# Attention scores masked before the exponential, from a score bank and an SBUF tile

## The chip, the cores and the metric

The kernel runs on one core of a Trainium2 chip. The metric is the device time of one execution in microseconds (us), the median of three runs.

## The reference, cut to what matters

```
scores = (1 / sqrt(64)) * q @ k.T                       # 4 batches, 8 heads, 576 x 576, head size 64
thresh = max(scores, axis=-1) - tau                     # tau = 0.02
scores = where(scores >= thresh, scores, -1e9)
attn   = exp(scores - max(scores))
attn   = attn / (sum(attn, axis=-1) + 1e-9)
x      = attn @ v                                       # then as 2304 x 512
x      = (silu(x @ w_gate) * (x @ w_val)) @ w_out       # inner size 1536
out    = ((x @ w1) * (x @ w2) @ w3) @ w_out2            # inner size 1024
```

All data are float32 (the weights come as 64-bit numbers). Products are made as sums of three matmuls over a high and a low part of each operand.

## The kernel before, in words

The function `attention` goes over 16 pairs of heads (4 batches x 4 pairs, `p`), and over 9 tiles `i` of 128 query rows by 576 keys in each, 144 tiles in all: tiles 0 to 3 are of the first head, 5 to 8 of the second, and tile 4 holds the last 64 rows of both. A loop over all tiles (L705) writes the stages of several tiles into each turn:

- `mm_scores` (L426): TensorE (PE) writes the scores of tile n + 2 into one of two score banks (`s_bank`, L91), with 4 matmuls (8 for tile 4).
- `el_max` (L475): VectorE (DVE) reads the bank of tile n + 1, multiplies by -1 (the operand `neg`), writes the negative scores to the tile's piece of `P` in SBUF and keeps the minimum, which is minus the row maximum, in `stat`. With this the bank is free.
- `el_thr` (L466): GpSimd (POOL) adds tau to these minima, for two tiles at a time in most cases.
- `el_exp` (L485): ScalarE (ACT) makes `E` = exp(score - max) from `P`; three buffers `E`.
- `el_mask` (L494), two tiles later (`N_THR`): DVE writes (P <= threshold) x E to `P` and the row sums to `sums`.

Between these, `some` (L693) spreads items of two queues. `main` holds the work on finished tiles: transposes of `P` on PE (`it_T`, `it_lq`, `it_kl`, `it_corner`, with `turn_p` at L326) and their split into a high and a low part (`evac_split`, L506, by one of three paths: with a subtraction on DVE at L520, with one by matmul on PE at L333, or with POOL at L101 and L104), and the value matmuls (`it_pv`, L569, matmuls at L579 and L584). `prep` holds the transposes of q and k for the next pair (`it_k`, `it_q`, `it_left`; the copies at L341 and L311, the low parts on DVE at L343); 0.125, the scale of the scores, goes into q there and, for the first pair, in `first` (L383). In pairs 3, 6 and 9 and in the last pair, conversion of weights (`conv_step`, L140 to L200) and loads of x come in too.

This order is not yet the order on an engine. The kernel is built with a scheduler (`schedule_with_timeline_sim`) that sorts the instructions of each engine by when it takes them to be ready; on the chip each engine then keeps its sorted order and waits on semaphores.

After the attention come the two feed-forward parts: conversion of weights, `glu_step` and the bilinear part, with nearly all matmuls at L830.

## Time and profile before

| | us |
|---|---|
| median of 3 runs | 1183.39 (1183.26 to 1184.7) |
| span of the profiled execution | 1178.8 |
| lowest run less this span | 4.5 |
| PE busy | 1113.3 (94%) |
| DVE busy | 750.1 (64%) |
| ACT busy | 578.1 (49%) |
| POOL busy | 439.7 (37%) |

The profile shows one execution. Its span is from the first to the last instruction; what lies around it is seen in the runs alone, and the lowest run stands in for the profiled execution's own time, which is not listed apart. PE is TensorE's matmuls, PEld its weight loads, SP the engine that issues DMAs. The shares are means over the whole span, in which the attention and the feed-forward parts differ. In the trace's rows an instruction stands as output<-inputs, with its line; a number in brackets, or after a bar, is the idle time of the engine before it and what ended that. PEclk is the granted TensorE clock as a share of full speed.

### The profile page before, as it was taken

Reading aid. Unit: us, or ns where it says so; the run is one execution under the profiler, and the core shown is the slowest. Engines: PE = TensorE matmul, PEld = TensorE weight load, DVE = VectorE, ACT = ScalarE, POOL = GpSimd, SP = SyncE. Lnnn points to the kernel's source line nnn. Section 1 sums busy time; section 2 is a strip of 40 time slices with the busy share of each in tenths; the row PEclk is TensorE's granted clock in tenths of the full one; section 3 lists DMA queues with packets and bytes.
Section 4 is the critical chain, followed back from the end, with each engine's and each line's share of the span. In section 5 each row is a group of like instructions: output and inputs, shape, how many; then the busy total and the mean of one; then the engine's idle time right before and its main releaser. Section 6 shows DMA issues by size and latency. Waiting matters only on the chain.

```text
span 1178.8 us, 16730 instructions
## 1 busy us (share of the span) xinstructions
PE 1113.3 (94%) x6044; PEld 952.0 (81%) x6044; DVE 750.1 (64%) x1320; ACT 578.1 (49%) x1041; POOL 439.7 (37%) x431
## 2 busy tenths in 40 slices
PE   6898879899988899999999999999899999999998
PEld 5787769788876778888888888888787888888886
DVE  7999898999886786665472655477891122522222
ACT  5787876888876455443232433344662231321111
POOL 4365454555444555443241432333242221321110
PEclk9999999999999999999999999999999999999999
DMA  8865674766555832221120120123330010100023
GB/s 189 194 146 131 145 177 112 167 147 137 121 175 141 257 99 87 89 72 55 35 71 19 54 72 19 52 92 102 113 108 18 1 36 1 36 1 1 1 60 101
DMA packets 105330, 107.07 MB, mean 91 GB/s; under 512 B 48288, under 2 KB 79648, under 8 KB 105248
## 3 DMA queue, kind: packets, MB, share of 16 engines
q1 hardware_dynamic: 105104, 106.01, 34.2%
q8 instruction: 47, 0.77, 0.3%
q14 instruction: 35, 0.29, 0.1%
q10 hardware_dynamic: 144, 0.00, 0.0%
HBM read 68.16 MB, written 14.23 MB: 70 GB/s over the span
## 4 chain that ended last, share of the span: by engine, by line
PE 64%; DVE 19%; DMA 8%; issue 3%; POOL 2%; SPq 2%; ACT 2%; DVEq 0%; ACTq 0%; POOLq 0%
PE t_bank L830 36%; PE s_bank L830 19%; DVE P L498 5%; DVE P L479 4%; PE t_bank L579 4%; PE s_bank L440 2%; DMA raw<-in_moe_w_dram 2%; DMA slot<-x_dram 1%; PE t_bank L326 1%; DVE slot L813 1%; DMA slot<-r_dram 1%; DVE tmp L158 1%; DVE tmp L146 1%; DVE AT L520 1%; DMA L<-qlo 1%
## 5 line engine op out<-in xcount | busy, mean ns | idle before, releaser
L830 PE MATMUL t_bank<-slot,slot 128*128 128x512 f32 (+1 forms) x2592 | 559.9, 371 | 5.6 <-DVE slot L813 1.8
L830 PEld LDWEIGHTS t_bank<-slot,slot 128*128 128x128 f32 x2592 | 457.5, 189 | 91.7 <-DVE slot L813 2.7
L830 PE MATMUL s_bank<-h,slot 128*128 128x512 f32 (+1 forms) x720 | 161.0, 371 | 7.4 <-DVE slot L877 4.2
L151 POOL TENSOR_TENSOR raw<-raw 128x512 int32<-128x512 int32 x76 | 83.9, 1104 | 189.0 <-ACT raw L150 165.3
L830 PEld LDWEIGHTS s_bank<-h,slot 128*128 128x128 f32 x720 | 126.4, 190 | 31.9 <-ACT tmp L914 3.2
L498 DVE SCALAR_TENSOR_TENSOR P<-P,stat,E 128x576 f32<-128x576 f32 x144 | 142.0, 999 | 11.8 <-POOL stat L471 10.6
L1062 DVE TENSOR_TENSOR tmp<-tmp,t_bank 128x512 f32<-128x512 f32 (+1 forms) x40 | 25.4, 634 | 178.3 <-PE t_bank L830 178.3
L488 ACT ACTIVATE E<-P,stat 128x576 f32<-128x576 f32 x144 | 113.6, 791 | 27.9 <-DVE P L479 25.2
L108 POOL TENSOR_TENSOR h<-tmp,h 128x512 fp32r<-128x512 f32 (+1 forms) x60 | 74.5, 1242 | 128.8 <-ACT h L107 128.6
L479 DVE TENSOR_SCALAR_CACHE_REDUCE P<-s_bank,neg 128x576 f32<-128x576 f32 x144 | 115.0, 808 | 10.3 <-PE s_bank L440 9.8
L1066 POOL TENSOR_TENSOR h<-tmp,h 128x512 fp32r<-128x512 f32 (+1 forms) x38 | 45.8, 1206 | 200.8 <-ACT h L1064 200.8
L440 PE MATMUL s_bank<-R,L 128*128 128x288 f32 x512 | 100.0, 317 | 19.3 <-DVE P L479 12.6
L830 PE MATMUL s_bank<-slot,h 128*128 128x512 f32 x432 | 106.6, 391 | 0.9 <-DVE slot L1052 0.8
L915 DVE TENSOR_TENSOR tmp<-tmp,t_bank 128x512 f32<-128x512 f32 (+1 forms) x60 | 37.9, 631 | 107.2 <-PE t_bank L830 100.5
L440 PEld LDWEIGHTS s_bank<-R,L 128*128 128x128 f32 x512 | 74.6, 191 | 33.8 <-DVE P L479 24.2
L326 PE MATMUL t_bank<-ident,P 128*128 128x128 f32 x640 | 91.4, 279 | 6.3 <-DVE klo L343 1.3
L830 PEld LDWEIGHTS s_bank<-slot,h 128*128 128x128 f32 x432 | 79.9, 188 | 18.3 <-DVE slot L1052 2.1
L158 DVE SCALAR_TENSOR_TENSOR tmp<-tmp,raw 128x512 f32<-128x512 f32 x76 | 69.5, 915 | 39.3 <-POOL raw L151 39.3
L877 DVE TENSOR_TENSOR slot<-s_bank,slot 128x1024 f32<-128x1024 f32 (+1 forms) x72 | 82.5, 1147 | 18.5 <-PE s_bank L830 16.5
L149 ACT ACTIVATE raw<-raw,ebias 128x512 int32<-128x512 int32 x76 | 58.0, 764 | 61.9 <-DVE tmp L146 48.2
L914 ACT ACTIVATE tmp<-t_bank 128x512 f32<-128x512 f32 (+1 forms) x60 | 33.3, 555 | 110.0 <-PE t_bank L830 104.3
L326 PEld LDWEIGHTS t_bank<-ident,P 128*128 128x128 f32 x640 | 74.3, 142 | 13.6 <-DVE klo L343 2.0
(103 smaller groups left out, 1397.8 us busy)
## 6 DMA issues: line engine op xcount, KB each, us to landing
raw<-in_moe_w_dram SPq DMA_DIRECT2D x32, 512.0 KB, 3.6
raw<-in_moe_w_out_dram SPq DMA_DIRECT2D x20, 512.0 KB, 3.6
x_dram<-xs SPq DMA_DIRECT2D x64, 144.0 KB, 2.4
L<-qlo SPq DMA_DIRECT2D x60, 128.0 KB, 2.4
...
```

Of the source, the lines that this page charges most:

```text
L108: nc.gpsimd.tensor_tensor(out=lo, in0=src, in1=f32(hi), op=ALU.subtract)
L149: nc.scalar.activation(out=a, in_=x, func=ACTF.Relu, scale=8.0, bias=ebias[:, 0:1])
L151: nc.gpsimd.tensor_tensor(out=a, in0=a, in1=x, op=ALU.subtract)
L158: nc.vector.scalar_tensor_tensor(out=f32(m), in0=f32(m), scalar=2.0 ** 20, in1=f32(a), op0=ALU.add, op1=ALU.mult)
L326: nc.tensor.matmul(bank[:, t * P:(t + 1) * P], lhsT=part, rhs=ident, is_transpose=True, start=(t == 0), stop=(t == len(parts) - 1),)
L440: nc.tensor.matmul(o, lhsT=lhs, rhs=R[:, c:c + HALF], start=(h == hs2[0] and e == 0), stop=(h == hs2[-1] and e == 1),)
L479: nc.vector.tensor_scalar(out=p_tile(p, i).rearrange("p (a c) -> p a c", a=2), in0=sb[:, :, 0:HALF], scalar1=neg, scalar2=None, op0=ALU.mu ...
L488: nc.scalar.activation(out=e, in_=p_tile(p, i), func=ACTF.Exp, scale=-1.0, bias=stats[p // HP][:, 0, c:c + 1],)
L498: nc.vector.scalar_tensor_tensor(out=t, in0=t, scalar=stats[b][:, 1, c:c + 1], in1=e, op0=ALU.is_le, op1=ALU.mult, accum_out=sums[b][:, c: ...
L579: nc.tensor.matmul(o, lhsT=vs[:, 4 * h + c, :, :].rearrange("p a d -> p (a d)"), rhs=AT[h][:, e, c, cs], start=(c == 0 and e == 0), stop=F ...
L830: nc.tensor.matmul(o, lhsT=lhs(a), rhs=rhs(c), start=(first and i == 0), stop=(last and i == 2))
L877: nc.vector.tensor_tensor(out=a, in0=s, in1=a, op=ALU.add)
```

## The change

- The scale 0.125 that goes into q becomes 0.125 / 1024 (`q_scale`, 0 where tau is negative), and is read from SBUF instead of being a constant. The score banks hold scores / 1024.
- `el_max`, `el_thr`, `el_exp` and `el_mask` give way to one function, `el_tile`, of four instructions in one chain. DVE multiplies the bank by -1024 into an SBUF tile (named `E`, two buffers) and keeps the minimum (L473). DVE adds tau to it (L477, 128x1). DVE compares the SBUF tile with that threshold and subtracts the bank from the result of 0 or 1, into `P` (L481): -s for what is kept, 1 - s for what is not, in units of 1024. ACT makes exp(-1024 x P - max), in place, which is 0 for what is not kept, and gives the row sums (L485).
- The bank is read last by L481. POOL has no part in this any more.
- A turn of the loop has `some(0.5)`, the tile, the scores of tile n + 2, `some(0.5)`. Work on a finished tile enters its queue in the turn of the tile, and not two turns later.

```diff
--- before.py
+++ after.py
@@ -19,7 +19,8 @@
 
 PASSES = ((0, 0), (0, 1), (1, 0))
 
-N_THR, N_E = 2, 3
+N_E = 2
+FAR = 1024.0
 
 N_U1, N_U2, N_U3, N_U4 = 3, 6, 9, 24
 N_TMP, N_BIG, N_HB = 6, 3, 3
@@ -85,7 +86,7 @@
     ident_r = const.tile([P, P], F32R, name="ident_r")
     minus_r = const.tile([P, P], F32R, name="minus_r")
     tau_sb = const.tile([P, 1], F32, name="tau_sb")
-    neg = const.tile([P, 1], F32, name="neg")
+    q_scale = const.tile([P, 1], F32, name="q_scale")
     ebias = const.tile([P, 2], F32, name="ebias")
 
     def s_bank():
@@ -360,7 +361,7 @@
                 stack(L[:, 2, :], hi, lo, 0)
                 stack(L[:, 3, :], lo, hi, 1)
 
-            turn(raws.pop((p, 0)), hi, lo, 0.125, then)
+            turn(raws.pop((p, 0)), hi, lo, q_scale, then)
 
         def it_k(p):
             L, R = qk_tiles(p)
@@ -418,7 +419,7 @@
                     nc.tensor.transpose(br[:, c:c + P], src, ident_r)
             lz = LZ.rearrange("p e (h c) -> p e h c", c=192)[:, :, :, 0:64]
             bv = bank.rearrange("p (e h c) -> p e h c", e=2, h=2)
-            scaled(lz, bv[:, :, :, 0:64], 0.125)
+            scaled(lz, bv[:, :, :, 0:64], q_scale)
             scaled(R[:, 512:640].rearrange("p (h c) -> p h c", h=2), bv[:, 1, :, 64:P])
             scaled(R[:, 2 * S:2 * S + 64], bv[:, 1, 1, 64:P])
 
@@ -463,41 +464,27 @@
                 sums[b] = wk.tile([P, NSM], F32, tag="sums", name="sums")
             return stats[b]
 
-        def el_thr(p, i):
-            st = stats[p // HP]
-            if i in (0, 2, 5, 7):
-                return
-            c = slice(col_of(p, i) - (i != 4), col_of(p, i) + 1)
-            nc.gpsimd.tensor_scalar(
-                out=st[:, 1, c], in0=st[:, 0, c], scalar1=tau_sb, scalar2=None, op0=ALU.add
-            )
-
-        def el_max(p, i, sb):
-            b = p // HP
-            st = stat(b)
-            c = col_of(p, i)
+        def el_tile(p, i, sb):
+            st = stat(p // HP)
+            c = slice(col_of(p, i), col_of(p, i) + 1)
+            src = sb[:, :, 0:HALF]
+            halves = lambda t: t.rearrange("p (a c) -> p a c", a=2)
+            t = wk.tile([P, S], F32, tag="E", name="E", bufs=N_E)
             nc.vector.tensor_scalar(
-                out=p_tile(p, i).rearrange("p (a c) -> p a c", a=2), in0=sb[:, :, 0:HALF],
-                scalar1=neg, scalar2=None, op0=ALU.mult, op1=ALU.min,
-                accum_out=st[:, 0, c:c + 1],
-            )
-
-        def el_exp(p, i):
-            c = col_of(p, i)
-            e = wk.tile([P, S], F32, tag="E", name="E", bufs=N_E)
+                out=halves(t), in0=src, scalar1=-FAR, scalar2=None,
+                op0=ALU.mult, op1=ALU.min, accum_out=st[:, 0, c],
+            )
+            nc.vector.tensor_tensor(
+                out=st[:, 1, c], in0=st[:, 0, c], in1=tau_sb, op=ALU.add
+            )
+            u = p_tile(p, i)
+            nc.vector.scalar_tensor_tensor(
+                out=halves(u), in0=halves(t), scalar=st[:, 1, c], in1=src,
+                op0=ALU.is_gt, op1=ALU.subtract,
+            )
             nc.scalar.activation(
-                out=e, in_=p_tile(p, i), func=ACTF.Exp,
-                scale=-1.0, bias=stats[p // HP][:, 0, c:c + 1],
-            )
-            return e
-
-        def el_mask(p, i, e):
-            b = p // HP
-            c = col_of(p, i)
-            t = p_tile(p, i)
-            nc.vector.scalar_tensor_tensor(
-                out=t, in0=t, scalar=stats[b][:, 1, c:c + 1], in1=e, op0=ALU.is_le, op1=ALU.mult,
-                accum_out=sums[b][:, c:c + 1],
+                out=u, in_=u, func=ACTF.Exp, scale=-FAR, bias=st[:, 0, c],
+                accum_out=sums[p // HP][:, c],
             )
 
 
@@ -654,13 +641,13 @@
         nc.scalar.dma_start(out=tau_sb, in_=tau.to_broadcast([P, 1]))
 
         nc.vector.tensor_scalar(
-            out=neg, in0=tau_sb, scalar1=0.0, scalar2=-1.0, op0=ALU.is_ge, op1=ALU.mult
+            out=q_scale, in0=tau_sb, scalar1=0.0, scalar2=0.125 / FAR, op0=ALU.is_ge, op1=ALU.mult
         )
         nc.vector.tensor_scalar(
             out=tau_sb, in0=tau_sb, scalar1=0.0, scalar2=None, op0=ALU.max
         )
         first(1, 1.0)
-        first(0, 0.125)
+        first(0, q_scale)
         split_left(0)
         it_left(0)
         load(0, (2,))
@@ -669,24 +656,19 @@
 
         tiles = [(p, i) for p in range(NP) for i in range(NTILE)]
         NS = len(tiles)
-        banks, es = {}, {}
+        banks = {}
 
         def stage_s(n):
             if n < NS:
                 banks[n] = mm_scores(*tiles[n])
 
-        def stage_max(n):
-            if n < NS:
-                el_max(*tiles[n], banks.pop(n))
-
-        def stage_mask(n):
-            if n >= 0:
-                p, i = tiles[n]
-                el_mask(p, i, es.pop(n))
-                if i == 4:
-                    main.extend(a_items(p))
-                if i == 8:
-                    main.extend(b_items(p))
+        def stage_el(n):
+            p, i = tiles[n]
+            el_tile(p, i, banks.pop(n))
+            if i == 4:
+                main.extend(a_items(p))
+            if i == 8:
+                main.extend(b_items(p))
 
         credit = [0.0, 0.0]
 
@@ -701,7 +683,6 @@
 
         stage_s(0)
         stage_s(1)
-        stage_max(0)
         for n, (p, i) in enumerate(tiles):
             b, hp = divmod(p, HP)
             if i == 0:
@@ -719,15 +700,10 @@
                     run_item(prep.popleft())
                 if p + 2 < NP:
                     prep.extend(split_items(p + 2))
-            some(0.4)
-            es[n] = el_exp(p, i)
-            stage_max(n + 1)
+            some(0.5)
+            stage_el(n)
             stage_s(n + 2)
-            el_thr(p, i)
-            some(0.3)
-            if n >= N_THR:
-                stage_mask(n - N_THR)
-            some(0.3)
+            some(0.5)
             if i == 4 and p in EARLY:
                 prep.extend([conv_step, conv_end])
             if n + NTILE == NS:
@@ -739,8 +715,6 @@
                     run_item(main.popleft())
                 qctx.close()
                 prep.extend(tail())
-        for n in range(NS - N_THR, NS):
-            stage_mask(n)
         while main or prep:
             for c in (0, 0, 0, 1):
                 qu = (main, prep)[c]
```

The scheduler makes a new order of all engines from this. Two places of it follow, both in the sixth pair of heads. On DVE, at tiles 2 to 4 of this pair, stood before (L479 is the maximum, L498 the mask, L520 and L343 are low parts for the matmuls):

```order
L498 SCALAR_TENSOR_TENSOR P0_1537,sums_1253<-P0_1537,stat_1252,E_1571 128x576
L479 TENSOR_SCALAR P2_1539,stat_1252<-s_bank_1574,neg_75 128x576
L498 SCALAR_TENSOR_TENSOR P1_1538,sums_1253<-P1_1538,stat_1252,E_1596 128x576
L479 TENSOR_SCALAR P3_1540,stat_1252<-s_bank_1599,neg_75 128x576
L498 SCALAR_TENSOR_TENSOR P2_1539,sums_1253<-P2_1539,stat_1252,E_1636 128x576
L479 TENSOR_SCALAR P4_1541,stat_1252<-s_bank_1639,neg_75 128x576
L498 SCALAR_TENSOR_TENSOR P3_1540,sums_1253<-P3_1540,stat_1252,E_1670 128x576
L520 TENSOR_TENSOR AT_106<-t_bank_1565,AT_106 128x512
L479 TENSOR_SCALAR P0_1537,stat_1252<-s_bank_1673,neg_75 128x576
L498 SCALAR_TENSOR_TENSOR P4_1541,sums_1253<-P4_1541,stat_1252,E_1697 128x576
L479 TENSOR_SCALAR P1_1538,stat_1252<-s_bank_1700,neg_75 128x576
L343 SCALAR_TENSOR_TENSOR klo_1583<-t_bank_1584,khi_1582 128x512
```

and now stands (L473 maximum, L477 tau, L481 mask):

```order
L473 TENSOR_SCALAR E_1695,stat_1310<-s_bank_1617 128x576
L473 TENSOR_SCALAR E_1746,stat_1310<-s_bank_1660 128x576
L477 TENSOR_TENSOR stat_1310<-stat_1310,tau_sb_74 128x1 x2
L481 SCALAR_TENSOR_TENSOR P2_1612<-E_1695,stat_1310,s_bank_1617 128x576
L481 SCALAR_TENSOR_TENSOR P3_1613<-E_1746,stat_1310,s_bank_1660 128x576
L473 TENSOR_SCALAR E_1783,stat_1310<-s_bank_1700 128x576
L477 TENSOR_TENSOR stat_1310<-stat_1310,tau_sb_74 128x1
L481 SCALAR_TENSOR_TENSOR P4_1614<-E_1783,stat_1310,s_bank_1700 128x576
L473 TENSOR_SCALAR E_1804,stat_1310<-s_bank_1751 128x576
L477 TENSOR_TENSOR stat_1310<-stat_1310,tau_sb_74 128x1
L481 SCALAR_TENSOR_TENSOR P0_1610<-E_1804,stat_1310,s_bank_1751 128x576
L473 TENSOR_SCALAR E_1838,stat_1310<-s_bank_1788 128x576
```

A mask stood behind maxima of one or two later tiles; now it is the third instruction on its own bank, and the maximum of the next tile but one is behind it, since that tile takes the same bank.

On PE, among the value matmuls of the pair before (L579 and L584, now L566 and L571; L440 and L441 are scores, L419 transposes the left-over rows of q and k, L334 subtracts by matmul), stood before:

```order
L579 MATMUL t_bank_1425<-AT_106,sp2_1215 128x288 x8
L584 MATMUL t_bank_1425<-ATL_107,VLZ0_110 128x288 x2
L440 MATMUL s_bank_1543<-R_1292,L_1291 128x288 x4
L579 MATMUL t_bank_1438<-AT_106,sp2_1215 128x288 x8
L584 MATMUL t_bank_1438<-ATL_107,VLZ0_110 128x288 x2
L579 MATMUL t_bank_1461<-AT_106,sp2_1215 128x288 x7
L579 MATMUL t_bank_1474<-AT_106,sp2_1215 128x288 x7
L440 MATMUL s_bank_1574<-R_1292,L_1291 128x288 x4
```

and now stands:

```order
L441 MATMUL s_bank_1660<-R_1328,L_1327 128x288 x4
L419 MATMUL t_bank_1709<-ident_r_72,qkls_952 128x128 x4
L566 MATMUL t_bank_1719<-AT_106,sp2_1507 128x288 x8
L571 MATMUL t_bank_1719<-ATL_107,VLZ1_111 128x288 x2
L566 MATMUL t_bank_1732<-AT_106,sp2_1507 128x288 x8
L571 MATMUL t_bank_1732<-ATL_107,VLZ1_111 128x288 x2
L334 MATMUL t_bank_1688<-AT_106,minus_r_73 128x512
L441 MATMUL s_bank_1700<-R_1328,LZ_108 128x288 x8
L566 MATMUL t_bank_1756<-AT_106,sp2_1507 128x288 x7
L441 MATMUL s_bank_1751<-R_1328,L_1327 128x288 x4
L566 MATMUL t_bank_1769<-AT_106,sp2_1507 128x288 x7
L566 MATMUL t_bank_1756<-AT_106,sp2_1507 128x288
```

Before, scores came behind 10 and behind 24 value matmuls. Now they come behind 20, then behind 7; behind the scores for s_bank_1751 follow 13 value matmuls in all and 8 transposes, and then the scores for s_bank_1788, into the bank of s_bank_1700.

## Rows read from the trace of the kernel before

**Rows 1.** The page, part 1: engine, busy us (share of the span) x instructions.
```profile
PE 1113.3 (94%) x6044; PEld 952.0 (81%) x6044; DVE 750.1 (64%) x1320; ACT 578.1 (49%) x1041; POOL 439.7 (37%) x431
```

**Rows 2.** Busy time by stretch: us, engines' busy us (x instructions), PEclk, DMA share, GB/s.
```profile
17.50:349.60 332.10, 296.87 (x2120) 267.16 (x2118) 307.11 (x696) 266.19 (x528) 169.45 (x199) 0.99 0.65 152
349.60:449.00 99.40, 87.92 (x431) 72.04 (x431) 75.22 (x101) 52.93 (x92) 50.00 (x40) 0.98 0.57 165
449.00:1178.80 729.80, 720.07 (x3449) 605.00 (x3448) 358.14 (x499) 252.62 (x411) 211.41 (x177) 1.00 0.16 51
```

**Rows 3.** Groups by line and shape, 17.5 to 349.6 us: busy us, mean ns | idle before.
```profile
L498 DVE SCALAR_TENSOR_TENSOR P<-P,stat,E 128x576 f32<-128x576 f32 x144 | 142.0, 999 | 11.8 <-POOL stat L471 10.6 <-ACT E L488 0.5 <-ACT xs L591 0.4
L479 DVE TENSOR_SCALAR_CACHE_REDUCE P<-s_bank,neg 128x576 f32<-128x576 f32 x144 | 115.0, 808 | 10.3 <-PE s_bank L440 9.8
...
L471 POOL TENSOR_SCALAR stat<-stat,tau_sb 128x2 f32<-128x2 f32 x64 | 34.7, 542 | 79.1 <-DVE P L479 75.5 <-DVE r L602 3.5
L520 DVE TENSOR_TENSOR AT<-t_bank,AT 128x512 fp32r<-128x512 f32 x46 | 31.3, 680 | 1.8 <-ACT AT L518 1.8
...
L498 DVE DVE_READ_ACCUMULATOR P<-P,stat,E 128x1 f32 x144 | 11.3, 78 | 0.0
L343 DVE SCALAR_TENSOR_TENSOR qlo<-t_bank,qhi 128x512 fp32r<-128x512 f32 x15 | 10.2, 681 | 0.0
...
L562 ACT CAST ATL<-t_bank 128x64 fp32r<-128x64 f32 x15 | 3.4, 228 | 0.4 <-PE t_bank L560 0.4
...
L563 DVE TENSOR_TENSOR ATL<-t_bank,ATL 128x64 fp32r<-128x64 f32 x15 | 3.2, 212 | 0.0
...
L813 DVE TENSOR_TENSOR slot<-tmp,slot 128x512 fp32r<-128x512 f32 x3 | 2.0, 680 | 0.0
```

**Rows 4.** Timeline around a long mask and a short one: start us, us, instruction.
```profile
160.07 1.79 POOL L104 TENSOR_TENSOR sp<-ld,sp 128x512 fp32r<-128x512 f32 x1
...
160.66 1.82 DVE L498 SCALAR_TENSOR_TENSOR P<-P,stat,E 128x576 f32<-128x576 f32 x1
...
263.43 0.81 DVE L498 SCALAR_TENSOR_TENSOR P<-P,stat,E 128x576 f32<-128x576 f32 x1
...
264.17 0.81 DVE L479 TENSOR_SCALAR_CACHE_REDUCE P<-s_bank,neg 128x576 f32<-128x576 f32 x1
```

**Rows 5.** Waits of DVE, PEld and POOL, 17.5 to 349.6: us, times, longest us.
```profile
DVE P L498 <- POOL stat L471: 10.6, 14, 2.1
DVE P L479 <- PE s_bank L440: 9.8, 10, 1.9
...
PEld s_bank L440 <- DVE P L479: 26.7, 48, 1.6
...
POOL stat L471 <- DVE P L479: 83.3, 46, 3.9
```

**Rows 6.** Timeline of DVE at the first tiles.
```profile
18.30 0.69 DVE L343 SCALAR_TENSOR_TENSOR qlo<-t_bank,qhi 128x512 fp32r<-128x512 f32 x1
18.91 0.81 DVE L479 TENSOR_SCALAR_CACHE_REDUCE P<-s_bank,neg 128x576 f32<-128x576 f32 x1
```

**Rows 7.** Timeline of DVE at the start.
```profile
7.18 0.15 DVE L659 TENSOR_SCALAR tau_sb<-tau_sb 128x1 f32<-128x1 f32 x1
7.24 0.42 DVE L395 SCALAR_TENSOR_TENSOR slot<-ld,slot 128x256 fp32r<-128x256 f32 x1
```

**Rows 8.** Timeline of DVE where L605 waits for L602.
```profile
183.18 0.18 DVE L602 TENSOR_SCALAR r<-sums 128x36 f32<-128x36 f32 x1
183.40 0.38 DVE L605 RECIPROCAL r<-r 128x36 f32<-128x36 f32 x1
```

**Rows 9.** Timeline of PE in the tile stretch.
```profile
154.26 1.22 PE L579 MATMUL t_bank<-AT,sp 128*128 128x288 f32 x8
...
158.23 1.03 PE L326 MATMUL t_bank<-ident,P 128*128 128x128 f32 x8
159.02 1.31 PE L440 MATMUL s_bank<-R,L 128*128 128x288 f32 x8
```

2 lines of the change are left out of this document (1 added, 1 removed).

## The prediction

> **What bounds the kernel now.** I read the page first: PE is busy 94% of the span [rows 1], yet that share mixes two regimes. The table by stretches separates them [rows 2]. From 449 us to the end PE is busy 720.07 of 729.8 us; the change touches nothing there. From 17.5 to 349.6 us, the stretch in which all 144 score tiles run, DVE is busy 307.11 of 332.1 us (92.5%), PE 296.87, ACT 266.19, POOL 169.45. So the tile stretch is set by DVE, with PE close behind. There are 16 head pairs of 9 tiles, so a pair takes 332.1/16 = 20.75 us, with 307.11/16 = 19.2 us of DVE in it.
>
> The groups by line tell what DVE does [rows 3]. The maximum (L479) is steady, 808 ns, although it reads the score bank. The mask (L498), over the same 576 columns, has a mean of 999 ns. Single masks show why [rows 4]: one takes 0.81 us alone, another 1.82 us, and starts while POOL subtracts SBUF tiles (L104, until 161.86) and ends 0.6 us after that. DVE instructions with one operand in a bank and one in SBUF (L520, L343) have means of 680 and 681 ns over 61 instructions, in the same stretch beside the same POOL work [rows 3]. So the long masks are a meeting of POOL and a DVE instruction with both tensors in SBUF. The waits add that DVE stood 10.6 us for the threshold from POOL (14 times) and 9.8 us for scores from PE, and that PE's weight loads stood 26.7 us for a score bank that a maximum had not yet read [rows 5].
>
> **The change, part by part.** Durations come from this one execution; its span is 4.6 us under the median of the runs, and I carry differences over to the median.
>
> *Mask.* The new mask reads one SBUF tile and one bank. If it meets POOL as little as L343 and L520 do, the excess of 0.999 - 0.81 = 0.19 us goes: 144 x 0.19 = 27 us. It has no accumulator read any more. L520 at 512 columns takes 0.680 us and L563 at 64 columns 0.212 [rows 3], which is 1.045 ns a column, so 576 columns take 0.747. The next instruction starts about 0.08 us before the end, as behind L343 [rows 6] (18.30 + 0.69, next at 18.91), so the new mask takes 0.67 us of DVE where an undisturbed old one takes 0.74 (263.43 to 264.17 [rows 4]): another 144 x 0.07 = 10 us.
>
> *Tau.* 144 additions of 128x1 come to DVE. L659, 128x1, starts at 7.18 and the next instruction at 7.24, 0.08 before L659 ends [rows 7]: 0.07 us each, 10 us. They also chain maximum, addition and mask through waits on DVE itself. L605, which waits for L602, starts at 183.40 where L602 ends at 183.36, while unchained instructions start 0.08 before the end [rows 8]: 0.11 us a chained start. In the new order 45 additions stand right behind their own maximum and 42 masks right behind their own addition: 87 x 0.11 = 10 us. The ends are 0 (all covered by other work) and 288 x 0.11 = 32 us; I take 10, from the order. The Trainium skill ("VectorE: DVE Perf Modes", The DRAIN you can't avoid) says that a next DVE instruction waits for the pipe to empty in any case and that a semaphore costs nothing on top; by it the term of 10 us would be 0. The rows differ: 0.08 before the end without a wait, 0.04 behind it with one.
>
> *DVE's account.* 27 + 10 - 10 - 10 = 17 us less work: 290 us, 18.1 a pair. The 10.6 us of standing for POOL's threshold go too.
>
> *POOL* loses its threshold instructions (34.7 us for those over two tiles [rows 3]) and with them the 83.3 us in which it stood before one for a maximum [rows 5], with splits of attention tiles behind it. I cost this at nothing: the longest wait of DVE for POOL in this stretch is the one for the threshold [rows 5], which is counted above, and PE had its weight loads wait for DVE, not for POOL.
>
> *ACT.* The exponential now also sums. No row shows that read on ACT. Below, DVE's own accumulator read is 0.078 us; above, a whole 64-column ACT instruction (L562) is 0.228 [rows 3]. I take 0.15, the middle, since it is an ACT instruction with nothing to stream: 144 x 0.15 = 22 us, 11 to 33. A scale read from SBUF on some 30 query copies costs ACT between nothing and, above, once more such a small instruction: 30 x 0.228 = 7 us; I take 3. ACT goes from 266 to about 291 of 332 us and still has 40 us of air. If that cover were gone, PE's transposes, which now wait for the exponential, would be late by up to 33/16 = 2 us a pair.
>
> *The score bank.* This is the price. A bank was free after the maximum; it is now free after maximum, addition and mask, which is 0.03 + 0.15 + 0.03 + 0.75 = 1 us later, and there are two banks. PE can no longer run ahead, and DVE has no backlog of three masks to work off while PE is away. I walk the piece of the new order shown above, with 0 at the issue of the scores for s_bank_1660. Eight score matmuls take 1.31 us to their end, and I take 0.55 for the issue of four; 30 value matmuls take 3.97 (154.26 to 158.23), 8 transposes 0.79 [rows 9].
> - PE: scores to 0.55, four transposes to 1.0, 20 value matmuls to 3.65, the subtraction by matmul to 3.9, scores of 1700 done at 5.2.
> - DVE: maxima of 1617 and 1660 from 0.3 to 1.9, additions to 2.1, both masks to 3.5; then nothing until 5.3: 1.8 us idle.
> - PE: 7 value matmuls, scores of 1751 done at 6.75, 13 value matmuls to 8.2, 8 transposes to 9.0, scores of 1788 done at 9.8. DVE is done with 1751 at 8.75: 1.1 us idle.
>
> So a pair has some 2.9 us of DVE idle at these two places, against 25/16 = 1.6 now. This pair carries five of the other DVE instructions of a pair; its DVE work is 17.2 us, so the average has 0.9 us more to fill idle places. If all of it fits, idle is 2.0; if none, 2.9. I take two thirds: 2.3. The pair then takes 18.1 + 2.3 = 20.4 us against 20.75: 16 x 0.35 = **5.4 us less**, 1178.0 from the median. The ends are 20.1 (10.4 us less) and 21.0 (4 us more). My times in the walk are good to some 0.2 us a pair, 3 us either way, and ACT's read may add 3: 1170 to 1193.
>
> Two edits cost nothing: two buffers for the SBUF tile are enough, since the mask that frees one is on the same engine, and the query scale waits for tau, which DVE waited for just before too, to make `neg`.
>
> **The rivals.** *Slower: the bank.* If DVE's idle is over 20.75 - 18.1 = 2.65 us a pair, the stretch gets longer. For it: the walked pair by itself has 2.9, and PE's work alone is 296.9/16 = 18.6 a pair, so both engines would have to interlock nearly without loss over two banks. Against: 27 us of the present DVE time come from POOL and fall irregularly, so the old order, made without them, stands still where the new one need not. With 2.9 us idle and a late transpose of 0.4 the pair is 21.4: 10 us more, 1194. Chance 0.28. *Slower by the bank's latency.* The Trainium skill ("VectorE: DVE Perf Modes", its errata table) gives a fixed 120 cycles for DVE reads from PSUM and 58 from SBUF, which speaks against a mask that reads the bank. In the rows 512 columns take 680 ns in both cases (L520 with a bank, L813 without [rows 3]). Were the mask 0.07 us longer all the same, as long as an undisturbed old one with its accumulator read, 10 us would come back: 1188. By the page's figures it would be an estimate of 62 cycles a mask. Chance 0.04.
> *No difference.* PE is so near that the saved DVE time turns into waits for PE, or the stretch from 349.6 to 449, where the weights' conversion and the loads of x follow their own pace (PE busy 87.92 of 99.4 us), gives it back: 1183, chance 0.18.
> *All of it.* If idle stays at 1 us, only the wait for PE and the rest of today's idle, the pair takes 19.1: 16 x 1.65 = 26 us less, 1157; PE at 18.6 hardly allows it. Chance 0.08.
> *Not what it says.* The mask may still meet POOL, by a way the rows of L343 and L520 don't show; then 27 us stay and the idle comes on top. This is in the 0.28.
>
> **How the numbers follow.** My forecast, 1178.0 with 1170 to 1181, has 0.42. With "all of it", faster by over 0.2% (2.4 us, about what a measurement of this kernel can tell from no change) has 0.50; within it 0.18; slower 0.28 + 0.04 = 0.32. The range of 8 in 10 goes from 1165, halfway to "all of it", to 1194, the bank's price; the forecast's own range stands beside it above.
>
> **What would show it.** The mask's mean at about 750 ns with none over 0.9; DVE busy near 290 us over the tile stretch; no wait of DVE for POOL's threshold; DVE's wait for scores up from 9.8 to some 35 to 45 us; ACT with an extra row of 0.08 to 0.23 us a tile; the last exponential some 5 us earlier than the last mask now (349.6), and the last 730 us unchanged. Masks of over 1 us, or waits for scores over 55 us, would make it wrong.

## The result and the profile after

The changed kernel takes **1191.42 us** (median; 1190.86 to 1192.23) against 1183.33 us for the kernel before on the same chip: ratio 1.0088, 95% interval 1.0061 to 1.0115. It is slower by 8 us by the medians (10 by the ratio); 5 us less were forecast.

The page, part 1 (engine, busy us, share of the span, instructions), and the table by stretches of the changed kernel: the tiles from the first maximum to the last mask, the hand-over, the feed-forward part.

```profile
PE 1124.1 (94%) x6044; PEld 955.8 (80%) x6044; DVE 753.5 (63%) x1319; ACT 596.5 (50%) x1187; POOL 384.4 (32%) x353
```
```profile
17.30:366.50 349.20, 309.46 (x2153) 273.58 (x2151) 308.89 (x700) 284.63 (x676) 115.42 (x123) 0.99 0.61 147
366.50:460.00 93.50, 83.97 (x395) 68.17 (x396) 77.20 (x97) 52.50 (x90) 49.34 (x39) 0.95 0.56 162
460.00:1190.40 730.40, 721.94 (x3451) 606.15 (x3449) 357.65 (x499) 252.71 (x411) 210.88 (x176) 0.99 0.16 52
```

Against [rows 2] the tiles take 349.20 us, not 332.10: 17 more. DVE, forecast at 290 us, has 308.89 of work (307.11 before), and its idle time went from 25 to 40 us. The hand-over is 6 us shorter than before (93.5 for 99.4), so 11.6 us of the 17 are left in the span (1190.4 for 1178.8), the last 730 us being as they were. The medians differ by 8 only, because the two profiled executions are not equally typical. That of the changed kernel is the slowest of its four runs (1192.23). In every run listed with its span, of all kernels here, the time is 1.7 to 3.1 us above the span; so a span of 1178.8 belongs to a time of 1180.5 to 1181.9 (an estimate from these runs), below the median of before, and the lowest run of 1183.26 was too high a stand-in for it.

The groups by line and shape in the tile stretch (busy us, mean ns | idle before):

```profile
L481 DVE SCALAR_TENSOR_TENSOR P<-E,stat,s_bank 128x576 f32<-128x576 f32 x144 | 114.5, 808 | 1.5
L473 DVE TENSOR_SCALAR_CACHE_REDUCE E<-s_bank 128x576 f32<-128x576 f32 x144 | 107.0, 752 | 32.9 <-PE s_bank L441 32.2
L477 DVE TENSOR_TENSOR stat<-stat,tau_sb 128x1 f32<-128x1 f32 x144 | 35.6, 256 | 1.6
L485 ACT ACTIVATION_READ_ACCUMULATOR P<-P,stat 128x1 f32 x143 | 28.9, 202 | 0.0
L344 DVE SCALAR_TENSOR_TENSOR qlo<-t_bank,q_scale,qhi 128x512 fp32r<-128x512 f32 x15 | 11.2, 746 | 0.6 <-ACT qhi L342 0.5
L342 ACT ACTIVATE qhi<-t_bank,q_scale 128x512 fp32r<-128x512 f32 x14 | 9.7, 694 | 8.1 <-PE t_bank L327 3.7 <-issue 2.6 <-ACT P L485 1.8
L344 DVE SCALAR_TENSOR_TENSOR klo<-t_bank,khi 128x512 fp32r<-128x512 f32 x14 | 9.5, 680 | 0.0
L342 ACT ACTIVATE khi<-t_bank 128x512 fp32r<-128x512 f32 x14 | 8.4, 600 | 0.1
```

The mask no longer meets POOL: mean 808 ns (none over 816) for 999 [rows 3]. But a new line stands beside it: 144 additions of a 128x1 tile, with a mean of 256 ns. The timeline shows two of them, one of which is among the dear ones (start us, us):

```profile
205.89 1.33 DVE L477 TENSOR_TENSOR stat<-stat,tau_sb 128x1 f32<-128x1 f32 x2
205.93 1.27 POOL L105 TENSOR_TENSOR AT<-tmp,AT 128x512 fp32r<-128x512 f32 x1
207.14 1.53 DVE L481 SCALAR_TENSOR_TENSOR P<-E,stat,s_bank 128x576 f32<-128x576 f32 x2
```

The two additions are through 0.02 us after POOL's instruction on SBUF tiles, and both masks stand behind them with both banks held. Of the 144 additions, 119 take 141 to 161 ns and 25 take 226 to 1281; each of the 25 ends 2 to 22 ns after a POOL instruction that ran beside it, and what they take above 154 ns is 15 us together. So the meeting with POOL moved from the mask to the addition, which also reads two SBUF tiles. The other additions cost little where the next instruction needs nothing from them, and more where the mask needs the sum:

```profile
43.40 0.16 DVE L477 TENSOR_TENSOR stat<-stat,tau_sb 128x1 f32<-128x1 f32 x1
43.48 0.68 DVE L507 TENSOR_TENSOR AT<-t_bank,AT 128x512 fp32r<-128x512 f32 x1
...
45.96 0.16 DVE L477 TENSOR_TENSOR stat<-stat,tau_sb 128x1 f32<-128x1 f32 x1
46.15 0.81 DVE L481 SCALAR_TENSOR_TENSOR P<-E,stat,s_bank 128x576 f32<-128x576 f32 x1
```

In the first case the next instruction starts 0.08 us after the addition did, before its end; in the second the mask starts 0.03 us behind its end. 42 masks stand so behind their own addition, and 45 additions start as late (0.035 us) behind the accumulator read of their maximum.

The waits in the same stretch (us, times, longest us):

```profile
DVE E L473 <- PE s_bank L441: 32.2, 34, 3.4
ACT P L485 <- DVE P L481: 23.4, 29, 3.4
...
PEld t_bank L327 <- ACT P L485: 12.4, 23, 1.6
PE s_bank L441 <- DVE P L481: 11.5, 14, 2.9
```

DVE waits 32.2 us for scores, for 9.8 before [rows 5]. The longest of these waits, in the timeline of PE and DVE:

```profile
195.83 1.53 DVE L481 SCALAR_TENSOR_TENSOR P<-E,stat,s_bank 128x576 f32<-128x576 f32 x2
195.90 1.23 PE L566 MATMUL t_bank<-AT,sp 128*128 128x288 f32 x8
196.97 0.43 PE L571 MATMUL t_bank<-ATL,VLZ 128*128 128x288 f32 x2
197.23 1.22 PE L566 MATMUL t_bank<-AT,sp 128*128 128x288 f32 x8
...
198.54 1.09 PE L566 MATMUL t_bank<-AT,sp 128*128 128x288 f32 x7
199.47 1.22 PE L441 MATMUL s_bank<-R,LZ 128*128 128x288 f32 x8
200.53 0.70 PE L441 MATMUL s_bank<-R,L 128*128 128x288 f32 x4
200.73 0.76 DVE L473 TENSOR_SCALAR_CACHE_REDUCE E<-s_bank 128x576 f32<-128x576 f32 x1 [3.37 <-PE s_bank L441]
```

The masks free the banks at 196.6 and 197.4, but PE is in a run of value matmuls until 199.5 and has no scores in store: DVE stands for 3.37 us. This is the walk of the prediction, at one place of one pair.

### The profile page after: what moved, and what is told of

Its sections match the earlier page's. It is cut to its first block, busy times and chain, and to the rows that moved or that the text cites. A ratio compares the mean times of both kernels' runs of the same rounds, so it can differ in the third digit from the quotient of the medians.

```text
span 1190.4 us, 16901 instructions
## 1 busy us (share of the span) xinstructions
PE 1124.1 (94%) x6044; PEld 955.8 (80%) x6044; DVE 753.5 (63%) x1319; ACT 596.5 (50%) x1187; POOL 384.4 (32%) x353
## 4 chain that ended last, share of the span: by engine, by line
PE 71%; DVE 15%; ACT 5%; DMA 3%; issue 3%; SPq 1%; POOL 0%; DVEq 0%; ACTq 0%; POOLq 0%
PE t_bank L804 37%; PE s_bank L804 19%; PE t_bank L566 5%; PE s_bank L441 5%; PE t_bank L327 3%; DVE E L473 3%; DVE P L481 2%; DMA raw<-in_moe_w_dram 2%; DVE slot L787 2%; ACT P L485 1%; DVE stat L477 1%; PE t_bank L571 1%; DVE raw L144 1%; DVE tmp L147 1%; DVE tmp L159 1%
## 5 line engine op out<-in xcount | busy, mean ns | idle before, releaser
L804 PE MATMUL s_bank<-h,slot 128*128 128x512 f32 (+1 forms) x720 | 164.1, 376 | 3.6 <-ACT h L108 2.9
L1036 DVE TENSOR_TENSOR tmp<-tmp,t_bank 128x512 f32<-128x512 f32 (+1 forms) x40 | 25.3, 633 | 178.2 <-PE t_bank L804 178.2
L473 DVE TENSOR_SCALAR_CACHE_REDUCE E<-s_bank 128x576 f32<-128x576 f32 x144 | 107.0, 752 | 32.9 <-PE s_bank L441 32.2
L485 ACT ACTIVATE P<-P,stat 128x576 f32<-128x576 f32 x144 | 113.5, 789 | 23.9 <-DVE P L481 23.4
L481 DVE SCALAR_TENSOR_TENSOR P<-E,stat,s_bank 128x576 f32<-128x576 f32 x144 | 114.5, 808 | 1.5
L441 PE MATMUL s_bank<-R,L 128*128 128x288 f32 x512 | 99.0, 317 | 16.0 <-DVE P L481 10.9
L327 PE MATMUL t_bank<-ident,P 128*128 128x128 f32 x640 | 98.4, 282 | 14.6 <-ACT P L485 7.8
L441 PEld LDWEIGHTS s_bank<-R,L 128*128 128x128 f32 x512 | 76.3, 195 | 27.5 <-issue 9.4
```

The costliest lines, as they stand in the source:

```text
L327: nc.tensor.matmul(bank[:, t * P:(t + 1) * P], lhsT=part, rhs=ident, is_transpose=True, start=(t == 0), stop=(t == len(parts) - 1),)
L441: nc.tensor.matmul(o, lhsT=lhs, rhs=R[:, c:c + HALF], start=(h == hs2[0] and e == 0), stop=(h == hs2[-1] and e == 1),)
L473: nc.vector.tensor_scalar(out=halves(t), in0=src, scalar1=-FAR, scalar2=None, op0=ALU.mult, op1=ALU.min, accum_out=st[:, 0, c],)
L481: nc.vector.scalar_tensor_tensor(out=halves(u), in0=halves(t), scalar=st[:, 1, c], in1=src, op0=ALU.is_gt, op1=ALU.subtract,)
L485: nc.scalar.activation(out=u, in_=u, func=ACTF.Exp, scale=-FAR, bias=st[:, 0, c], accum_out=sums[p // HP][:, c],)
L804: nc.tensor.matmul(o, lhsT=lhs(a), rhs=rhs(c), start=(first and i == 0), stop=(last and i == 2))
```

## The experiments

All kernels were run beside the kernel before, which came to 1180.8 to 1182.6 us; times are medians. The experiments ran on several chips: differences between them are of medians, and counted from the kernel before on the same chip they come out up to 3 us smaller or larger. In the chip's order nothing follows the source alone: the scheduler sorts each engine again whenever an instruction's form changes. With the numbers of the names left out and equal neighbours put together, PE's matmuls in the trace of the kernel before are 768 rows; the comparisons below say where an experiment changed many of them.

**What the addition costs.** Four kernels: the addition with tau as a scalar (one SBUF tensor in place of two), no addition, the same addition behind the mask, and the kernel before with this addition alone.

```
e1_add_one_sbuf  -  nc.vector.tensor_tensor(out=st[:, 1, c], in0=st[:, 0, c], in1=tau_sb, op=ALU.add)
                 +  nc.vector.tensor_scalar(out=st[:, 1, c], in0=st[:, 0, c], scalar1=tau_sb, scalar2=None, op0=ALU.add)
e2_no_add        -  nc.vector.tensor_tensor(out=st[:, 1, c], in0=st[:, 0, c], in1=tau_sb, op=ALU.add)
                    mask: scalar=st[:, 1, c]  ->  scalar=st[:, 0, c]
e8_add_behind    as e2_no_add, with the tensor_tensor written behind the mask
e5_add_alone     kernel before: in el_thr, gpsimd.tensor_scalar for two tiles -> vector.tensor_tensor for each tile
```

> The changed kernel, with tau added by a tensor-scalar instruction: one SBUF tensor and tau as its per-partition scalar, instead of two SBUF tensors of one column. Theory port (the 25 of 144 additions that took 0.23 to 1.28 us met POOL on SBUF, 15 us in all, each in the chain that holds a score bank): all additions at 0.14 to 0.17 us, DVE busy 15 us less in the tile stretch, the kernel 7 to 13 us faster than the changed one, 1178 to 1184. Theory bank (holding the bank through the mask costs the time by itself): additions short, but DVE stands longer for scores instead, 1187 to 1192. If this form meets POOL as well: nothing changes, 1190 to 1193.

> The changed kernel without the addition: the mask takes the maximum itself as its threshold, so tau is left out of the result. Theory port: as with the short addition, and some 10 us less of DVE besides: 1172 to 1182. Theory bank: the bank is held about 0.2 us less in each tile, a fifth of what the chain added: 1186 to 1190. Theory ACT (the sum on ScalarE makes the exponential late for PE's transposes): no more than 3 us, 1188 to 1192.

> The changed kernel with the add of tau moved behind the mask, its result unused; the mask compares with the maximum itself, so tau is left out of the threshold. VectorE's instructions stay the same in number and kind; only the time for which the bank of scores is held gets shorter, by the add. Without any add the time was 1165.7, with it in the chain 1191.4. Theory A (the chain: an instruction between the two reads of the bank costs through the hold): 1168 to 1182, wait for scores 25 us or less. Theory B (VectorE's work: an add costs the same wherever it stands): 1186 to 1193, VectorE busy 305 to 312 us, wait for scores within 6 us of the changed kernel's 32.

> The kernel before with one part of the change alone: tau is added on VectorE, one 128x1 add of two SBUF operands per tile, instead of on GpSimd for pairs of tiles; the order, the mask and the exponential stay. It lies behind the release of the bank of scores. Work on VectorE: 144 adds of about 0.21 us are 30 us more, and the mask's meeting with GpSimd's add (up to 27 us above 0.81 us for each mask) goes in part, since other GpSimd work goes on. Theory B (the work of VectorE sets the stretch of tiles): busy time 305 to 325 us, and the time follows it: 1178 to 1192. Theory A (the hold sets it, work outside of it is covered by idle time): 1172 to 1182, VectorE's idle time falls by as much as its busy time rises.

e1_add_one_sbuf 1190.62 us, ratio to the kernel before 1.0074 (1.0049 to 1.0099). e2_no_add **1165.73**, 0.9864 (0.9831 to 0.9897). e8_add_behind 1182.69, 0.9982 (0.9963 to 1.0002). e5_add_alone 1208.03, 1.0194 (1.0147 to 1.0241). The additions, then the tile stretch by the table of stretches, for e1_add_one_sbuf:

```profile
L477 DVE TENSOR_SCALAR stat<-stat,tau_sb 128x1 f32<-128x1 f32 x144 | 27.3, 208 | 1.3
```
```profile
16.70:361.30 344.60, 310.22 (x2153) 273.57 (x2151) 299.82 (x700) 283.46 (x676) 115.69 (x123) 0.99 0.63 150
```

for e2_no_add:

```profile
17.30:337.80 320.50, 301.23 (x2145) 271.12 (x2144) 278.75 (x555) 279.20 (x674) 113.53 (x122) 0.99 0.67 159
```

for e8_add_behind:

```profile
16.90:354.50 337.60, 307.58 (x2152) 273.24 (x2152) 303.81 (x700) 283.99 (x677) 114.50 (x123) 0.98 0.64 152
```

and for e5_add_alone (mask and addition):

```profile
L496 DVE SCALAR_TENSOR_TENSOR P<-P,stat,E 128x576 f32<-128x576 f32 x144 | 128.2, 895 | 6.6 <-ACT E L486 6.3
...
L469 DVE TENSOR_TENSOR stat<-stat,tau_sb 128x1 f32<-128x1 f32 x144 | 39.9, 282 | 0.1
```
```profile
17.20:367.00 349.80, 300.71 (x2091) 269.99 (x2090) 323.51 (x840) 263.41 (x522) 125.53 (x120) 0.97 0.62 144
```

Without the addition DVE has 278.75 us of work for 308.89: the addition is worth 30 us of DVE (20 were forecast), and 26 us of time, more than any of its ranges allowed. In e1_add_one_sbuf no addition is longer than 217 ns, so POOL's 15 us are gone. But with tau as a scalar each addition takes DVE longer, 0.124 us from its start to the next start for 0.072 (medians of those with an unchained follower), some 7 us. So 9 us of DVE's work went, idle time rose from 40.3 to 44.8, and the time is the same within the intervals, in the range of theory bank. Behind the mask the same addition costs 17 us (1182.69 against 1165.73), in the chain another 9. In the kernel before, where its result is needed by nobody for two tiles, it costs 25 us, more than both ranges allowed: DVE's work rises by 16.4 and its idle time stays (26.3 for 25.0), so the stretch is 18 us longer, and the rest lies behind the last mask (842.3 us from there to the end, for 829.2). Theory B, the work, fits the stretch of e5_add_alone; the time of e8_add_behind lies between the ranges of A and B. The place in the chain has the smaller part, and its 9 us are hardly larger than what a new order alone may give (below). For this part speaks DVE's idle time: 33.8 us with the addition behind the mask, and 40.3, 44.8, 43.3 and 45.2 us with it in the chain (the changed kernel, e1_add_one_sbuf, and e7_order and e17_query_immediate below).

**The bank.** The mask reads the SBUF tile twice, so the bank is free after the maximum; once with the addition, once without.

```
e3_bank_free     mask: in1=src -> in1=halves(t);  exp: scale=-FAR -> scale=1.0
e12_bank_no_add  the same on e2_no_add
```

> The changed kernel, with the mask reading the SBUF tile for both operands (exp then takes it with scale 1), so that the bank is free after the maximum; scores under the threshold are then not dropped. Theory bank: DVE's wait for scores falls from 32 us to under 15 us; the masks meet POOL again (mean near 1.0 us, 27 us more of DVE), so 1183 to 1190. Theory port alone: nothing is gained from the bank, the masks' 27 us come on top: 1195 to 1215.

> The changed kernel with both suspects taken away: no add (tau is left out, the mask compares with the maximum itself), and the mask reads the SBUF tile twice instead of the bank, so that the bank is free after the maximum (scores below the threshold are then not dropped from the sum). The mask with two SBUF operands will meet GpSimd as the kernel before's did. Alone, the missing add gave -25 us, the free bank -9 us. If the two are separate costs: 1154 to 1162. If they are one cost, the hold of the bank (theory A): 1163 to 1172, since one of them is enough to take it away. If VectorE's busy time sets it (theory B): 1163 to 1175, with busy time near 290 us, because the mask's meetings give back 10 us or more.

e3_bank_free 1182.63 us, 1.0008 (0.9989 to 1.0027); e12_bank_no_add 1173.65, 0.9917 (0.989 to 0.9945). Mask and stretch of e3_bank_free:

```profile
L481 DVE SCALAR_TENSOR_TENSOR P<-E,stat 128x576 f32<-128x576 f32 x144 | 131.7, 932 | 0.4
```
```profile
16.70:353.50 336.80, 298.39 (x2129) 270.45 (x2128) 320.40 (x697) 280.21 (x673) 127.64 (x122) 0.98 0.63 150
```

and of e12_bank_no_add:

```profile
L478 DVE SCALAR_TENSOR_TENSOR P<-E,stat 128x576 f32<-128x576 f32 x144 | 137.0, 971 | 0.5
```
```profile
17.40:336.00 318.60, 292.74 (x2118) 268.63 (x2117) 293.22 (x549) 276.45 (x668) 131.74 (x121) 0.98 0.66 155
```

The held bank is what makes DVE wait: free, DVE's idle time is 16.4 us in place of 40.3, and 25.4 in place of 41.8 without the addition. But the mask with two SBUF tensors meets POOL again (932 and 971 ns), 11.5 and 14.5 us more work. With the addition that nets 9 us for the free bank, 12 us in the stretch. Without it the stretches are nearly level, 318.6 us with the bank free and 320.5 with it held; the 8 us by which the held bank is the faster lie behind the last mask (835.4 us from there to the end with the bank free, 827.3 with it held). Of the ranges for e12_bank_no_add only theory B's holds 1173.65, with DVE's work at 293.22 us. So reading the bank in the mask loses in the stretch while the addition is there, and about breaks even without it.

**ACT and the order.** The sum left off ACT; other work moved by a tenth of a tile; the query's scale an immediate.

```
e4_no_sum            -  accum_out=sums[p // HP][:, c],      +  nc.vector.memset(sums[b], 1.0) for each block
e7_order             some(0.5), some(0.5)  ->  some(0.4), some(0.6)
e17_query_immediate  q_scale  ->  0.125 / FAR at its three uses
```

> The changed kernel without the sum on ScalarE: the exponential keeps its form but accumulates nothing, and the row sums are set to one ahead of each block, so the division by the row sum is left out. It takes away the 144 accumulator reads of 202 ns, 29 us of ScalarE. Theory A (chain and add: what counts is the time in which a bank of scores is held, and VectorE's own work; ScalarE is behind the bank's release): within 4 us of the changed kernel's 1191, VectorE's wait for scores still 28 to 36 us. Theory C (ScalarE: the reads make the exponentials late, the transposes wait for them and the scores stand behind the transposes in TensorE's order): 1172 to 1182, the 19 us of transposes waiting on the exponential fall below 8 us, and VectorE's wait for scores falls below 20 us.

> A control: the changed kernel, with the items of the two queues spread 0.4 before and 0.6 behind a tile instead of 0.5 and 0.5. No work changes, only the order that the scheduler makes. If the loss lies in an unlucky order: over 5 us to one side. If it lies in the tile's instructions: 1188 to 1195, additions over 0.2 us 20 to 30 times again, DVE waiting 25 to 40 us for scores.

> The changed kernel with the query's scale as an immediate (0.125/1024) instead of the pointer. Theory Q: the pointer costs the changed kernel too, 1180 to 1187. Rival (in the changed kernel no score waits for the query's transfer, its waits fall at the tiles 4 to 6 of a pair behind the products for the output): 1188 to 1193.

e4_no_sum 1187.02 us, 1.0034 (1.0017 to 1.0052); e7_order 1193.66, 1.0091 (1.0061 to 1.0122); e17_query_immediate 1191.07, 1.0086 (1.0053 to 1.0118). 29 us off ACT give 4 us, and DVE still waits 29.5 us for scores, as theory A has it: ACT is not the bound, and its share of the loss is some 4 us. The three kernels with the addition in the chain and another order (e1_add_one_sbuf, e7_order, e17_query_immediate) come to 1190.6 to 1193.7, so the 8 us are not one unlucky order.

**Parts of the change on the kernel before.** The changed kernel's maximum is 56 ns shorter than [rows 3] has it, since its factor is an immediate; could the kernel before have that alone?

```
e6_immediate       max: scalar1=neg -> scalar1=-1.0;  q's scale: 0.125 -> q_scale (128x1 pointer)
e13_max_immediate  the first alone            e14_query_pointer  the second alone
e15_no_read        mask: accum_out left out; sums set to 1
e22_before_shift   some(0.4), some(0.3), some(0.3)  ->  some(0.3), some(0.3), some(0.4)
```

> The kernel before with another small part of the change alone: the maximum's factor is an immediate (-1) instead of the pointer neg, and the query's scale is a pointer instead of an immediate. The rows of the changed kernel show the maximum at 752 ns instead of 808: 144 x 56 ns = 8 us less on VectorE, against some 3 us that the query's pointer adds on ScalarE and VectorE. Theory B (VectorE's work sets the stretch): 1173 to 1179. Rival (the idle time beside the scores takes it up, as it took up most of the shorter add): 1180 to 1184.

> The kernel before with the immediate in the maximum and nothing else: the other part. VectorE loses 144 x 56 ns = 8 us. Theory Q: 1173 to 1181. Rival M: 1187 to 1193, VectorE's waits for scores near 30 us at the first tiles of the pairs.

> The kernel before with the query's scale as a pointer (0.125 in a 128x1 tile) and nothing else: one of the two parts of the run with the immediate maximum, which was 10 us slower than before though VectorE had 13 us less to do. Theory Q (the pointer: 0.06 us longer on VectorE and 0.09 us on ScalarE in each split of the query, ahead of the transfers that stack it, so that the first scores of a pair wait for the transfer): 1187 to 1193, waits of the scores for the query's transfer 10 us or more. Rival M (a shorter maximum is what disturbs the order): 1180 to 1184, those waits near before's 5 us.

> The kernel before with the mask's accumulator read away: the mask sums nothing, the row sums are set to one ahead of each block, so the division by the row sum is left out. It measures the term of the prediction for the read that the change takes off VectorE: 144 x 0.07 us = 10 us. Theory B (VectorE's work sets the stretch): 1169 to 1176. Rival (the read lies below the next instruction's start and below idle time): 1179 to 1184.

> The kernel before with a tenth of a tile's other work moved from ahead of the exponential to behind the mask (0.3, 0.3, 0.4 in place of 0.4, 0.3, 0.3); no instruction is added or taken away. It asks what a shift of the order alone costs the kernel before. If small shifts cost what the query's pointer and the immediate maximum did (theory S: the times of before hang on how the tiles' pieces and the products happen to fall together): 1185 to 1192. Rival (those two costs belong to their instructions): 1179 to 1184.

e6_immediate 1191.18 us, 1.0084 (1.006 to 1.0108); e13_max_immediate 1188.03, 1.0058 (1.0037 to 1.0079); e14_query_pointer 1190.07, 1.0092 (1.0061 to 1.0124); e15_no_read 1179.01, 0.9981 (0.9958 to 1.0004); e22_before_shift 1182.28, 1.0008 (0.9991 to 1.0026). The first three miss every expectation of a gain: both parts lose, each alone. e13_max_immediate lies in rival M's range and e14_query_pointer in theory Q's, so neither theory has both; and the scores' wait for the query's transfer, Q's reason, is 8.0 us in e14_query_pointer, less than the 10.3 in e13_max_immediate, which has no pointer there (PE's waits). For e13_max_immediate, the maximum and the waits:

```profile
L479 DVE TENSOR_SCALAR_CACHE_REDUCE P<-s_bank 128x576 f32<-128x576 f32 x144 | 106.3, 749 | 25.3 <-PE s_bank L440 25.3
```
```profile
DVE P L479 <- PE s_bank L440: 25.3, 21, 5.1
```

The maximum is 59 ns shorter, as meant, and DVE waits 25.3 us for scores in place of 9.8. The tile stretch and what follows it, for e13_max_immediate and then e14_query_pointer:

```profile
17.10:349.40 332.30, 293.32 (x2119) 267.23 (x2117) 295.14 (x696) 265.12 (x527) 164.47 (x200) 0.99 0.65 151
349.40:1181.10 831.70, 810.34 (x3881) 678.04 (x3880) 432.43 (x600) 306.10 (x503) 261.02 (x215) 0.99 0.22 65
```
```profile
17.70:349.90 332.20, 291.32 (x2076) 262.23 (x2076) 304.00 (x694) 265.04 (x521) 164.38 (x197) 0.99 0.60 147
349.90:1186.80 836.90, 817.29 (x3924) 685.29 (x3922) 432.94 (x604) 308.50 (x509) 262.50 (x216) 0.99 0.22 66
```

Both stretches are as long as before (332.1 us): the 12 us of work that e13_max_immediate saves turn into waiting. What these profiles show of the loss lies behind the last mask, where the kernel before takes 829.2 us. (The profiled execution of e13_max_immediate is the fastest of its ten runs, 1183.04 us, and holds only part of its loss.) The two kernels do not have the order of the kernel before: 677 rows have to be put in or taken out to turn PE's 768 rows into those of e13_max_immediate, 312 for e14_query_pointer, 16 for e15_no_read. e22_before_shift was meant to price such a shift and did not: its order is that of the kernel before on every engine, so it only measures that kernel again. That a new order is what costs e13_max_immediate and e14_query_pointer 6 to 8 us is thus argued, not shown. It does mean that differences below some 8 us between kernels of different order (e1, e3, e4 and e8 against the changed kernel) carry their sign by the account of work and idle time, not by the time alone. e15_no_read, in which PE's order is nearly that of before, is the cleanest price: without DVE's accumulator read DVE has 4 us less work (303.27 us), where 10 were forecast, and the time is not clearly shorter (2 us by the medians, with an interval that holds 1; the profiled stretch is 332.5 us for 332.1).

**No addition at all, with the reference's threshold.** First on the kernel before: the threshold is taken on the exponential. Then on the changed kernel: the first read takes tau off the scores, so that its maximum is the threshold; the mask compares the bank with it; the exponential's bias is made beside the mask, on POOL or on ACT.

```
e11_thr_on_exp   el_thr left out;  mask: in0=t, scalar=stats..., is_le  ->  in0=e, scalar=e_tau, is_ge;  and e6_immediate
e18_thr_exp_imm  the same with q's scale 0.125
e20_bias_pool    max:  scalar1=-FAR, mult, min            ->  scalar1=tau_sb, subtract, max
                 add:  vector.tensor_tensor(st1 = st0 + tau)  ->  gpsimd.tensor_scalar(st1 = st0 * -FAR)
                 mask: in0=t, scalar=st1, in1=src, is_gt   ->  in0=src, scalar=st0, in1=t, is_lt
                 exp:  bias=st0                            ->  bias=st1;     tau_sb = max(tau, 0) / FAR
e21_bias_act     the same with scalar.mul(st1 = st0 * -FAR)
```

> The kernel before with the immediate maximum, and with the threshold taken on the exponential: the mask keeps E where E is at least exp(-tau), one scalar for all tiles, so that no add of tau is left on any engine, VectorE or GpSimd. The mask reads E twice from SBUF and stays two tiles behind, the bank is free after the maximum, and the sum stays on VectorE. Theory B: VectorE loses 8 us on the maxima and, with 43 us of GpSimd's work gone, part of the mask's meetings (mean 999 to 900-960 ns, another 6 to 14 us): 1160 to 1172. Rival (GpSimd's other work then comes denser and meets the masks as often): mask mean 980 to 1010 ns, 1172 to 1180.

> The kernel before with the immediate maximum and the threshold taken on the exponential (no add of tau on any engine), the query's scale an immediate as before. With the query's pointer it came to 1181.8. Theory Q: 1169 to 1177, faster than both kernels. Rival M: 1178 to 1185.

> The changed kernel without an add on VectorE, and with the reference's threshold: the first read takes tau off the scores (t = score - tau, the pointer in place of the factor, 0.056 us longer), so that its maximum is the threshold itself; the mask compares the bank with it and takes t off; GpSimd makes the exponential's bias from the maximum (one 128x1 product per tile, about 0.3 to 0.5 us beside the mask's 0.81). The run that left tau out came to 1165.7; the pointer adds 144 x 0.056 = 8 us on VectorE. Theory (the add on VectorE, inside the chain, was the loss): 1168 to 1178, VectorE busy 285 to 292 us. Rival (GpSimd takes its work in order and stands up to 12 us behind ScalarE and TensorE, so the exponentials and with them the transposes come late): 1185 to 1230, ScalarE's waits for the bias over 30 us.

> As the run before it, but ScalarE makes the bias itself, ahead of the exponential and beside the mask: 144 x about 0.2 us = 29 us more on ScalarE. Taking the 29 us of accumulator reads off ScalarE gave 4 us, so adding as much should cost about that: 1170 to 1181, VectorE busy 285 to 292 us. Rival (ScalarE, then near 310 us, becomes the bound): 1182 to 1195, transposes' waits for the exponential over 25 us.

e11_thr_on_exp 1181.79 us, 1.0005 (0.9985 to 1.0026), and e18_thr_exp_imm 1178.88, 0.9972 (0.9952 to 0.9993), the first above both of its ranges, the second in rival M's: without POOL's 43 us of additions the mask still has a mean of 981 and 966 ns. e20_bias_pool is at 1173.12, 0.9924 (0.9907 to 0.9941), in its theory's range, and e21_bias_act at **1168.42**, 0.9883 (0.9868 to 0.9897), just below its own: 14 us below the kernel before, 23 below the changed one. The rows of e21_bias_act:

```profile
L473 DVE TENSOR_SCALAR_CACHE_REDUCE E<-s_bank,tau_sb 128x576 f32<-128x576 f32 x144 | 115.8, 813 | 35.7 <-PE s_bank L441 35.1
L479 DVE SCALAR_TENSOR_TENSOR P<-s_bank,stat,E 128x576 f32<-128x576 f32 x144 | 115.2, 813 | 1.5
L483 ACT ACTIVATE P<-P,stat 128x576 f32<-128x576 f32 x143 | 114.8, 805 | 9.2 <-DVE P L479 8.3
L477 ACT ACTIVATE stat<-stat 128x1 f32<-128x1 f32 x144 | 32.5, 234 | 6.5 <-DVE E L473 5.7
```
```profile
17.30:343.10 325.80, 303.37 (x2154) 272.29 (x2152) 286.21 (x556) 294.65 (x819) 113.90 (x123) 0.99 0.66 157
```

DVE's work is 286.21 us, its idle time 39.6, as much as in the changed kernel (40.3): the held bank costs what it did, and the 23 us are the addition's. In e20_bias_pool ACT waited for POOL's bias three times, 4.4 us in all, far from the rival's 30. Three orders with the held bank and no addition on DVE (with e2_no_add) lie at 1165.7 to 1173.1, four with it at 1190.6 to 1193.7. (e4_no_sum, which has the addition but not the sums on ACT, is at 1187.0.) This settles that the addition on DVE is the cause. How much of it comes through DVE's work, and how much through the longer hold of the banks, is not separated.

## Why the prediction was wrong

By its own steps, us of the tile stretch:

| step | forecast | measured |
|---|---|---|
| mask no longer meets POOL | -27 | -27: none over 816 ns |
| mask without accumulator read, start to start 0.74 to 0.67 | -10 | -2: 0.727 (median over masks with a direct follower) |
| maximum with an immediate factor | not listed | -8: 144 x 56 ns |
| addition, from its start to the next start | +10: 0.07 each | +10: 0.07 each (median of 75 short ones with an unchained follower) |
| its chained starts | +10: 87 x 0.11 | +10: 42 masks and 45 additions, 0.11 to 0.12 us later than an unchained start |
| its meeting with POOL | not listed | +15: 25 additions, above 154 ns each |
| other DVE work inside the stretch | 0 | +5: 78.4 for 73.9 us, sum of the durations |
| DVE's work | -17 | +2 by the table of stretches (+3 by the terms, of which some 3 of the chained starts are idle time) |
| DVE's idle time | +12 (2.3 a pair) | +15 (2.5 a pair) |
| stretch | -5 | +17 |
| hand-over | 0 | -6 in the span |

**The step that failed is DVE's account, and in it the addition's meeting with POOL, which the prediction put at nothing.** What it did price came out: 0.07 us from L659 [rows 7] for the addition itself, and 0.11 for each of 87 chained starts. But the addition reads two SBUF tensors, and one of 128x1 stands for POOL as long as a large one: 25 additions did, and that is 15 us, half of the 30 by which DVE's work falls without the addition (308.89 - 278.75). The prediction used that meeting for the mask and did not ask it of the addition. The Trainium skill ("SBUF — State Buffer", Who interferes with whom) says that a DVE instruction with two SBUF inputs contends with a GpSimd instruction that reads SBUF; the rows agree, with 25 additions of up to 1281 ns, and none over 217 ns with a single SBUF tensor. What this meeting alone is worth in time stays open: e1_add_one_sbuf takes it away, but pays 7 us for the pointer, and is not clearly faster.

**The mask's pitch** was worked out from L520 and L563, which have no scalar read from SBUF. The mask reads its threshold as one, and takes 808 ns, not 747: the 10 us for the read were 2. The same effect, with the other sign, was missed in the maximum (752 for 808), and pays it back.

**The bank** was right in kind and nearly in size: idle time 2.5 us a pair for 2.3, wait for scores 32.2 us for "35 to 45". The rival "slower: the bank" gave 1194, near what came, but by idle time over 2.65 a pair, which did not come; it was the work, 308.89/16 = 19.3 a pair for 18.1, that made the pair 21.8 us. That 2.5 is so near 2.3 is in part luck: in the kernels with a held bank and 279 to 300 us of DVE's work (e1_add_one_sbuf, e2_no_add, e17_query_immediate, e20_bias_pool, e21_bias_act) the idle time is 39.6 to 45.2 us, 2.5 to 2.8 a pair. So in e1_add_one_sbuf and e17_query_immediate, with DVE's work at 300 us, below the 307 of before, the time is still 9 to 10 us above before. It is luck, too, that 1191 lies inside the wide range of 1165 to 1194: its upper end was the price of idle time at the bank.

**The page on chained starts.** By the Trainium skill's rule that a semaphore costs nothing on top ("VectorE: DVE Perf Modes", The DRAIN you can't avoid) the chain's term was 0, by the forecast 10. The rows bear out the forecast: a mask that needs the sum starts 0.035 us behind the end of its addition, an instruction that needs nothing from it 0.07 to 0.08 before that end.

**ACT** had 28.9 us of reads for 22 and the cover held, apart from some 4 us. **POOL** lost its threshold, and no wait of DVE for it is left. The last exponential ended at 369.3 us, 20 us later than the last mask of before (5 us earlier were forecast), and the last 730 us were unchanged. That a change of the tile stretch comes out whole at the end was not so: a third of the 17 us was given back where the feed-forward part begins.
